# Norms and casts of three batches dealt anew between GpSimd and ScalarE, with a new written-out order

## The chip, the cores and the metric

The kernel runs on one core of one Trainium2 chip. The metric is device time in microseconds of one execution. The time of a kernel is the median of several runs; a profile is one further execution, taken by the hardware profiler.

The engines are named as the profile names them: PE is TensorE (matmuls; PEld is its loading of weights), DVE is VectorE, ACT is ScalarE, POOL is GpSimd, and SP is SyncE, which here only issues transfers. Each engine runs its instructions strictly in the order in which the program gives them, and waits at the head of its queue until what the next instruction needs is there.

## The reference, cut to what matters

```
# attention with forget gates: 8 batches, 8 heads, 576 positions, head size 64
scores = q @ k.T / 8
cum    = cumsum(log(clip(f, 1e-4, 1)))
scores = where(causal, -1e9, scores + cum[:, None] - cum[None, :])
attn   = exp(scores - max(scores))
attn   = attn / sum(attn)                  # the "norm" of this text
x      = attn @ v                          # -> 4608 tokens x 512
# bilinear feed-forward network
out    = ((x @ w_a) * (x @ w_b)) @ w_out   # 512 -> 1536 -> 512
```

All inputs and the output are fp32. The kernel works in fp16 with fp32 sums.

## The kernel before

**Work and tiles.** Heads are taken in pairs. A pair of heads of one batch is numbered `t` (0 to 31, four pairs to a batch), half a batch (two pairs) is `u` (0 to 15). The 576 rows of a pair fall into blocks of 128, `i` = 0 to 3, and a last block of 64 rows, `i` = 4. Scores are computed in groups: `groups = [(1, 0), (2,), (3,), (4,)]`, so that the operations `qk0` to `qk3` each make the scores of one group for one `u`.

**A pair's way.** The scores of a group are written by TensorE into PSUM (`sc`, L403). In batches 0 to 2 (`DIRECT = 3`) the decay is added by matmuls, VectorE takes the maximum of each row (`do_max`, L490) and ScalarE the exponential straight from PSUM (`do_exp`, L546 and L552), with its row sum; the next group reuses the banks of `sc`, so it waits for these exps. From batch 3 on VectorE adds the decay and takes the maximum in one instruction (`do_decay`, L514), reading a table that GpSimd masks (`mask_copy`, L464; `mask_tail`, L470; `mask_last`, L475). VectorE then takes the reciprocal of the sums (`do_recip`). The norm (`do_norm`, L569) multiplies the probabilities of one block and one head by it, in place, in the tile `PA` (blocks 0 to 2) or `PB` (3 and 4); `norm0` to `norm4` are its operations by block, two each, and one for block 4. Batch 0 isn't normed so: there the reciprocals are put across by small matmuls (`rhi` and `rlo` split them into two halves, `rmm` and `rev` spread them over rows) and multiplied in when the product with the values is read out. After its norms the tile is transposed by a transfer that SyncE issues (`do_tr`, L607, giving `PTA` and `PTB`), and TensorE multiplies it with the values (`pv`, `pv4`, `pve`; L635 to L660). In batch 0 TensorE does the transposes (`ptr`), and VectorE or ScalarE copy them out (`evp`).

**Inputs.** Queries, keys and values are loaded as fp32 by SyncE, cast to fp16 (`caqk`, `cav`), and queries and keys are transposed by VectorE (`tqk`, L304). In batch 0 the casts are shared out; from batch 1 on all are GpSimd's.

**Feed-forward.** Tokens are taken in blocks of 256 to 512. For each of 12 slices of the inner size TensorE makes `psa` and `psb` (L929), ScalarE or VectorE copies `psa` out (`aev`), and VectorE multiplies (`mul`, L945); `pso` (L954) is the second product, copied out by `ocopy` and stored by `sto` (L969). These matmuls are put between those of attention.

**What sets the order.** The program first lists all its work as 2307 operations, each with its function, the engines that it may run on (a string of letters: A for ScalarE, D for VectorE, P for GpSimd, S for SyncE) and what it depends on:

```
nm = op("P", f"norm{i}", lambda e, i=i, h=h: do_norm(e, t, i, h), [rc])
```

Then two texts decide: `ORDER` gives the sequence of the operations' numbers, and with it each engine's queue, and `CHOICE` gives one letter to each operation that has more than one engine to choose from. `laid_out` reads both. 40 matmuls without use (`fill`, L179) are part of the order; they keep TensorE at work.

Of the kernel before, what the change touches and what calls it, by code (L numbers as in the profile page):

```python
# [37 lines left out]
def kernel(  # L38
# [11 lines left out]
    nc = tc.nc  # L50
# [256 lines left out]
    def batch_inputs(b):  # L307
# [4 lines left out]
        for which, part, gm in items:  # L312
            gate = qk_ops[(2 * (b - 1) + gm // 4, gm % 4)][-1:] if b >= EARLY else []
            if which == "v":
                m, w = len(part), sbw[part[0]]
                ld = op("S", "ldv", lambda _, part=part: load_v(b, part), size=8 * m * w)
                ld.after.extend(gate)
                nu = take(ld, "n32")
                ca = op(("P" if 0 in part else "APD") if b == 0 else "P", "cav", lambda e, part=part: cast_v(e, b, part), [ld, o_p], 512 * m)
# [15 lines left out]
            for lo, hi in (((0, 5), (5, TW)) if b == 0 else ((0, TW),)):  # L335
                ca = op("APD" if b == 0 else "P", "caqk",
# [226 lines left out]
    def do_norm(e, t, i, h):  # L563
        st = T[("st", t)]
# [4 lines left out]
        ENG[e].tensor_scalar(out=p, in0=p, scalar1=st[:, c:c + 1], scalar2=1.0, op0=MUL, op1=MUL)  # L569
# [128 lines left out]
    def softmax(t, g, qk, sc, rows, st_users, pu, norms):  # L698
# [4 lines left out]
        for i in groups[g]:  # L703
# [67 lines left out]
            for h in range(1 if i == 4 else 2):  # L771
                nm = op("P", f"norm{i}", lambda e, i=i, h=h: do_norm(e, t, i, h), [rc])
# [261 lines left out]
    for t0, n in [(0, 256), (256, 256), (512, 256), (768, 384)] + [(1152 + 512 * n, 512 if n < 6 else 384) for n in range(7)]:  # L1034
# [3 lines left out]
        42-44 0 8 33 10 71 34 11 66 22 32 21 4 39 1 23 64 54 14 45-47 25 20 48 55-57 36 41 72-74 49 19 9 65  # L1038
        50 67-69 51 40 3 58 75-77 18 70 78 61 62 79-81 96 109 113 83 84 24 110 82 111 27 5 13 97 101 26 2 59
# [5 lines left out]
        198 199 173 178 150 180 179 174 176 175 286 230 185 287-289 299 214 305 87 88 200 177 300 306 207  # L1045
# [3 lines left out]
        369 233 238 229 195 1623 443 1624-1626 196 239 363 1627 1630 1632 279 370 1628 1629 236 371 1631 280  # L1049
        1634 1633 208 1636 364 365 258 284 275 259 281 285 244 245 237 388 393 209 372 389 290 292 394 291  # L1050
        282 283 445 1635 406 1638-1640 390 35 246 395 1637 1641 260 311 448 324 330 312 318 396 444 210 28
        201 202 247 366 261 325 326 211 1642 1643 314 264 266 267 327 320 319 265 1644 252 446 332 331 391
        333 313 321 322 373 315 203 204 349 356-358 392 329 253 350 352 351 367 250 449 1647 374 1648-1650
        347 251 303 1652 1654 375 382 353 1645 1653 1655 348 1656 1658 1657 1660 384 1662 328 1659 1661 1664
        1665 453 383 376 1663 1666-1668 1670 378 1669 1672 377 447 385 1674 1673 1671 1675 397 409 410 704
# [3 lines left out]
        476 478 495 477 386 504 454 455 506 505 1651 411 458 412 1700-1702 420 421 334 467 501 304 479 1703  # L1059
# [8 lines left out]
        615 552 607 547 1760 1763 1761 526 527 535 558-560 586 588 1764-1766 587 1768 1769 1772 1773 561 598  # L1068
        589 1774 1770 622 634 557 636 1771 1775 1776 1778 1777 1780 1781 667 674 642 546 675 708 604 1782
        1783 541 592 669 676 677 1784 1786 569 1779 581 641 580 594 1785 1787-1790 1792 563 643 562 593 635  # L1070
        591 585 590 605 606 608 678 644 595 645 646 637 668 609 638 640 639 1762 1793 1796 623 626 1794 602
        1795 627 1798 628 630 1791 647 670-672 631 648 650 681 683 1797 1799 1800 797 1801 1804 649 682 1802
        1803 651 652 684 620 632 655 1806 680 1805 679 1807 709 656 794 653 688 689 654 700 603 1808 1810
        1809 629 798 685 612 1812 1813 1816 1811 633 624 1817 657 658 1814 1815 1767 1818 1821 610 1822 690
        617 710 660 662 687 621 661 663 693-695 659 664 691 1819 673 696 697 686 702 712 724 732 731 757 765
        759 767 1823 1826 665 1827 726 764 1824 666 701 625 766 799 758 768 760 699 1828 698 692 703 795
# [12 lines left out]
        911 1906 966-968 925 926 915 927 914 918 931 933 916 917 935 904 959 961 1910 1010 919 969 970 936  # L1089
        1893 971 1014 972 1911 937 1912 1011 1915 973-975 1913 1914 938 920 1897 943 1003 939 960 1015 934  # L1090
        940 942 1012 928 976 977 1000 941 1916 1919 1921 944 905 1917 1920 1922 945 1016 912 913 909 1918
        921 946 1923 948 949 947 978-980 1898 990 1924 981 982 1927 1888 988 950 1100 951 952 1925 984 1929
# [97 lines left out]
```

## Time and profile before

| | |
|---|---|
| median of 3 runs | 403.02 us (402.19 to 403.34) |
| profiled execution | 401.62 us, of which the span from first to last instruction is 399.8 us |
| granted TensorE clock | 0.994 of full speed |
| busy PE, DVE, ACT, POOL | 385.3, 313.6, 252.1, 238.4 us |
| transfers | 78.21 MB, mean 196 GB/s |

A matmul's end is modelled in the profile, since matmuls overlap, so a busy TensorE need not be one at its peak. In the rows that name an instruction, `out<-in` are the tiles that it writes and reads, and the text in brackets or behind the last bar says for how long the engine had been idle before it and what ended that. A line such as L140 or L144 is that of the helper `cast` and stands for many uses.

### The profile page before, as it was taken

The numbers are of one execution on the slowest core, as the hardware profiler recorded it, in microseconds if no ns is written. First come the engines' busy times: TensorE is split into PE (matmuls) and PEld (weight loads), VectorE is DVE, ScalarE is ACT, GpSimd is POOL, SyncE is SP. The second block draws the span as 40 slices with busy tenths as digits, with TensorE's granted clock in tenths as the row PEclk, the third lists the DMA queues.
The fourth block names the chain that finished last, engine by engine and source line by source line (L and its number), as shares of the span: only waits on it lengthen the run. The fifth ranks groups of instructions, "written<-read, shape, count | busy, mean of one in ns | idle before, by whom it ended". The sixth has DMA issues, their size and how long they took to land.

```text
span 399.8 us, 10965 instructions
## 1 busy us (share of the span) xinstructions
PE 385.3 (96%) x4000; PEld 206.5 (52%) x4000; DVE 313.6 (78%) x915; ACT 252.1 (63%) x760; POOL 238.4 (60%) x401
## 2 busy tenths in 40 slices
PE   8888999999998999999999999999999999999996
PEld 2466876758655444444444454444444444444553
DVE  7999997978788979978988888899978891653361
ACT  6888986666565767767785677666868683201210
POOL 6461558896396877885886939768877563000000
PEclk9998999999999999999999999999999999999999
DMA  7999989999979999999999798999999827101102
GB/s 266 261 223 235 206 174 249 225 187 180 313 214 198 235 236 261 226 294 200 295 229 266 153 281 200 230 247 218 267 195 222 178 41 152 52 2 71 61 2 80
DMA packets 148310, 78.21 MB, mean 196 GB/s; under 512 B 130592, under 2 KB 133408, under 8 KB 148256
## 3 DMA queue, kind: packets, MB, share of 16 engines
q1 hardware_dynamic: 144560, 72.79, 78.9%
q0 software_dynamic: 3696, 4.72, 7.2%
q8 instruction: 31, 0.51, 0.5%
q14 instruction: 23, 0.19, 0.1%
HBM read 49.69 MB, written 9.58 MB: 148 GB/s over the span
## 4 chain that ended last, share of the span: by engine, by line
PE 62%; DMA 8%; DVE 8%; ACT 7%; POOL 7%; issue 5%; SPq 0%; POOLq 0%; DVEq 0%; ACTq 0%
PE pso L954 17%; PE psa L929 16%; PE psb L929 15%; PE sc L403 7%; DMA PTB<-PB 4%; DVE S L514 3%; POOL PB L569 3%; ACT PA L552 2%; DMA q<-in_q_dram 2%; POOL PA L569 2%; PE pv L635 1%; DMA spread<-cum_d 1%; DVE st L490 1%; PE pv L647 1%; ACT PB L552 1%
## 5 line engine op out<-in xcount | busy, mean ns | idle before, releaser
L929 PE MATMUL psa<-xT,wa 128*128 128x512 f16 (+2 forms) x528 | 115.6, 342 | 1.0 <-ACT a L140 0.5
L929 PE MATMUL psb<-xT,wb 128*128 128x512 f16 (+2 forms) x528 | 116.1, 343 | 0.0
L954 PE MATMUL pso<-wout,ht 128*128 128x512 f16 (+1 forms) x444 | 98.0, 374 | 0.0
L945 DVE TENSOR_TENSOR ht<-psb,a 128x512 f16<-128x512 f32 (+2 forms) x132 | 75.5, 588 | 22.6 <-PE psb L929 14.3
L569 POOL TENSOR_SCALAR PA<-PA,st 128x128 f16<-128x128 f16 (+2 forms) x150 | 70.1, 480 | 36.6 <-DVE st L561 27.4
L514 DVE CUSTOM_DVE_ANT_0 S<-sc,spread 128x128 f32<-128x128 f32 (+3 forms) x160 | 86.1, 569 | 4.3 <-PE sc L403 2.2
L552 ACT ACTIVATE PA<-S,st 128x256 f16<-128x256 f32 (+2 forms) x120 | 60.0, 502 | 21.8 <-DVE st L514 19.8
L929 PEld LDWEIGHTS <-wa 128*128 128x128 f16 x528 | 50.5, 98 | 44.8 <-issue 4.1
L140 ACT CAST a<-psa 128x512 f16<-128x512 f32 (+2 forms) x88 | 44.9, 517 | 44.9 <-PE psa L929 43.4
L929 PEld LDWEIGHTS <-wb 128*128 128x128 f16 x528 | 50.1, 98 | 42.0 <-issue 2.4
L954 PEld LDWEIGHTS <-ht 128*128 128x128 f16 x444 | 41.8, 98 | 47.4 <-issue 1.5
L569 POOL TENSOR_SCALAR PB<-PB,st 128x512 f16<-128x512 f16 (+1 forms) x78 | 54.5, 713 | 10.7 <-DVE st L561 6.6
L490 DVE TENSOR_REDUCE st<-sc 128x2 f32<-128x512 f32 (+8 forms) x68 | 46.6, 726 | 7.3 <-PE sc L403 7.2
L403 PE MATMUL sc<-kT,qT 32*128 32x128 f16 (+5 forms) x960 | 40.3, 268 | 4.0 <-ACT PA L552 2.1
L552 ACT ACTIVATE PB<-S,st 128x512 f16<-128x512 f32 x40 | 28.5, 714 | 6.0 <-DVE st L514 6.0
L403 PEld LDWEIGHTS <-qT 32*128 32x128 f16 (+1 forms) x960 | 18.7, 95 | 23.8 <-issue 13.5
L144 POOL CAST nv<-v 128x1024 f16<-128x1024 f32 (+1 forms) x24 | 21.3, 894 | 15.7 <-DMA v<-in_v_dram 15.7
L140 ACT COPY osb<-pso 128x512 f32<-128x512 f32 (+1 forms) x23 | 13.0, 571 | 25.1 <-PE pso L954 22.9
L144 DVE CAST a<-psa 128x256 f16<-128x256 f32 (+2 forms) x44 | 24.2, 551 | 5.7 <-PE psa L929 5.1
L561 DVE RECIPROCAL st<-st 128x2 f32<-128x2 f32 x128 | 18.1, 157 | 12.1 <-ACT PB L552 5.9
L142 POOL TENSOR_SCALAR q<-q 128x1152 f16<-128x1152 f32 (+1 forms) x15 | 20.9, 1395 | 8.8 <-DMA q<-in_q_dram 8.8
L552 ACT ACTIVATE PA<-sc,st 128x256 f16<-128x256 f32 (+2 forms) x42 | 19.6, 494 | 8.5 <-DVE st L490 3.6
(107 smaller groups left out, 485.3 us busy)
## 6 DMA issues: line engine op xcount, KB each, us to landing
spread<-cum_d SPq DMA_DIRECT2D x20, 576.0 KB, 6.0
out_dram<-osb SPq DMA_DIRECT2D x35, 256.0 KB, 3.6
q<-in_q_dram SPq DMA_DIRECT2D x15, 576.0 KB, 6.8
k<-in_k_dram SPq DMA_DIRECT2D x15, 576.0 KB, 7.5
v<-in_v_dram SPq DMA_DIRECT2D x32, 256.0 KB, 6.9
wout<-in_moe_w_out_dram POOLq DMA_DIRECT2D x3, 512.0 KB, 8.9
wa<-in_moe_w_a_dram POOLq DMA_DIRECT2D x1, 1024.0 KB, 11.7
v<-in_v_dram SPq DMA_DIRECT2D x8, 128.0 KB, 5.3
```

What stands on the lines that cost most here:

```text
L140: nc.scalar.copy(out=out_, in_=in_)
L142: ENG[e].tensor_scalar(out=out_, in0=in_, scalar1=0.125, scalar2=1.0, op0=MUL, op1=MUL)
L144: ENG[e].tensor_copy(out=out_, in_=in_)
L403: nc.tensor.matmul(out=dst, lhsT=lhsT, rhs=rhs, start=start, stop=stop, skip_group_check=True)
L490: nc.vector.tensor_reduce(out=m if i == 4 else st[:, 2 * i:2 * i + 2][:, h:h + 1] if isinstance(x, list) else m, in_=y, axis=AXX, op=MAX, ...
L514: nc.vector.tensor_tensor_reduce(out=o, in0=x, in1=y, scale=-1.0, scalar=3e38, op0=ADD, op1=MIN, accum_out=m)
L552: nc.scalar.activation(out=p_blocks(t, i)[:, :, h, :], in_=x.rearrange("p (j k) -> p j k", k=128), func=EXP, scale=sign, bias=st[:, c:c + ...
L561: nc.vector.reciprocal(out=st[:, 20 + 2 * i:22 + 2 * i], in_=st[:, 10 + 2 * i:12 + 2 * i])
L569: ENG[e].tensor_scalar(out=p, in0=p, scalar1=st[:, c:c + 1], scalar2=1.0, op0=MUL, op1=MUL)
L929: nc.tensor.matmul(out=o, lhsT=w16[:, db, 128 * fb:128 * fb + 128], rhs=tokens(db, t0, n), start=(db == 0), stop=(db == 3))
L945: nc.vector.tensor_tensor(out=ht[:, 0:n], in0=T.pop(("psb", t0, fb))[:, 0:n], in1=T.pop(("a16", t0, fb))[:, 0:n], op=MUL)
L954: nc.tensor.matmul(out=o, lhsT=T[("ht", t0, fb)][:, 128 * tb:128 * tb + 128], rhs=wout16[:, fb, c], start=(fb == 0), stop=(fb == 11))
```

## The change

The norms of batches 1 and 2 may now run on ScalarE or GpSimd, and so may the casts of batches 1 to 3. `do_norm` gets a branch for ScalarE: a copy with the reciprocal as its scale. `ORDER` and `CHOICE` are new texts; the orders agree from a point in batch 5 on. By the letters of `CHOICE`:

- 16 of the norms are given to ScalarE: for `t` = 4, 5, 6, 7 one, two, three and three; for `t` = 8, 10 and 11 two, two and three. By block they are two `norm0`, five `norm1`, four `norm2`, four `norm3` and one `norm4`.
- Of the casts, one goes to ScalarE: the last 64 rows of the values of batch 3.
- 15 copies of `psa` go from ScalarE to VectorE and 6 from VectorE to ScalarE. Of the read-outs of products with the values (`ev`, `ev4`, `eve`) five go from ScalarE to VectorE and eight the other way. Two `ocopy` change places in each direction, two `rev` go to ScalarE and one to VectorE, one `evp` goes to VectorE. Of the halves of reciprocals of batch 0, three `rlo` and two `rhi` go from GpSimd to VectorE, two `rhi` from VectorE to ScalarE, one from VectorE and one from ScalarE to GpSimd.
- In the order of the transfers one store comes ahead of the first query load of batch 3, and the two decay loads of batch 3 (`ldb`) change places.

```
-                ca = op(("P" if 0 in part else "APD") if b == 0 else "P", "cav", ...
+                ca = op(("P" if 0 in part else "APD") if b == 0 else "PA" if b < 4 else "P", "cav", ...
...
-                ca = op("APD" if b == 0 else "P", "caqk",
+                ca = op("APD" if b == 0 else "PA" if b < 4 else "P", "caqk",
...
-        ENG[e].tensor_scalar(out=p, in0=p, scalar1=st[:, c:c + 1], scalar2=1.0, op0=MUL, op1=MUL)
+        if e == "A":
+            nc.scalar.activation(out=p, in_=p, func=COPY, scale=st[:, c:c + 1])
+        else:
+            ENG[e].tensor_scalar(out=p, in0=p, scalar1=st[:, c:c + 1], scalar2=1.0, op0=MUL, op1=MUL)
...
-                nm = op("P", f"norm{i}", lambda e, i=i, h=h: do_norm(e, t, i, h), [rc])
+                nm = op("PA" if b < 3 else "P", f"norm{i}", lambda e, i=i, h=h: do_norm(e, t, i, h), [rc])
...
     ORDER = """   (new text; the first 1418 of 2307 places differ)
...
     CHOICE = """   (new text)
```

More of the change, by code (lines that the diff above doesn't have):

```diff
@@ L318, in batch_inputs @@
                 nu = take(ld, "n32")
-                ca = op(("P" if 0 in part else "APD") if b == 0 else "P", "cav", lambda e, part=part: cast_v(e, b, part), [ld, o_p], 512 * m)
+                ca = op(("P" if 0 in part else "APD") if b == 0 else "PA" if b < 4 else "P", "cav", lambda e, part=part: cast_v(e, b, part), [ld, o_p], 512 * m)
                 nu.append(ca)
@@ L1051 @@
[L1051 to L1055, printed above, removed]
[3 rows of a table removed]
@@ L1072 @@
[L1072 to L1076, printed above, removed]
@@ new lines @@
+        115 101 114 98 103 99 11 102 33 10 20 6 121 122 66 83 84 126 128 268 146 124 104 127 16 123 24 90
+        134 138-140 147 135 269 226 136 151 152 227 153 149 89 116 100 14 31 155 105 137 112 148 117 129 156
+        157 141 142 164 158 160 162 125 161 143 91 169 212 213 254 255 240 170 171 118-120 271 165 272 144
+        145 241 234 235 166 167 52 53 262 263 130-133 92 273 63 248 249 276 220 106-108 221 93 182-184 18
+        1594 190 191 1596 1595 1597 1598 1600 270 1599 168 1602 1604 150 1601 216 217 159 197 205 206 7 198
@@ new lines @@
+        199 173 178 180 179 286 1603 1606 174-176 287 293 1607 185 186 299 305 214 187 95 288 289 294 300 85
[4 rows of a table added]
+        371 236 364 365 237 366 285 258 259 282 244 245 368 292 388 346 348 1633 393 394 389 1634-1636
+        1638-1640 1637 1641 390 391 210 211 202 260 261 311 324 330 312 332 326 325 372 246 331 318 283 445
[3 rows of a table added]
+        384 1655 1659-1661 1664 1665 376 1666 1662 1663 1668 1670 341 456 383 1667 1669 385 387 1672 1674
+        1673 378 377 379 1671 1675 321 397 402 406 403 398 399 1676 1678 342 1677 1680-1682 316 1684 303
@@ new lines @@
+        1679 1683 404 417 422 460 423 1685 1688 492 498 1686 1687 1689 1690 493 494 499 500 705 464 470 465
+        471 472 1692 1693 1691 1694 1695 38 409 410 466 405 310 1696-1698 408 28 501 467 469 381 416 413 414
+        495 618 400 1651 461 476 478 477 1699 504 505 450 506 420 507 380 457 458 1700 1701 479 407 1702 411
+        412 473 462 1703 454 474 482 483 510 455 434 317 1705-1707 386 511 329 335 1708 421 323 322 424 427
+        428 463 433 436 437 435 415 418 419 502 438-440 401 441 512 451 452 17 484 486 488 514 1710-1712
@@ new lines @@
+        646 700 611 661 663 659 691 692 1822 694 696 664-666 1767 799 695 697 712 757 724 732 725-727 734
+        701 699 698 703 1819 795 796 1823 1826-1828 625 759 765 767 1831 1824 764 766 1833 728 730 729 758
+        731 733 768 769 1832 1835 1836 1834 713 716 1837 717 720 714 715 721 1838-1840 735 737 736 738 739
+        760 761 740 771 772 805 806 741 1841 1842 718 719 802 803 816 773 742-744 722 762 810 745 746 707
+        774-776 1843 778 779 711 763 777 1844 1847 1845 1846 1848 770 747 748 1849 749 1850 812 723 750 1820
@@ new lines @@
+        1080-1083 1052 1053 1013 1084 1085 1102 1017 1054 1952 1005 1086 1087 1953 1954 1957 1076 1029 1025
[5 rows of a table added]
+        1136-1138 1115 1140 1141 1133 1164 1166 1169 1989 1201 1212 1213 1142 1196 1170 1171 1210 1991 1993
+        1992 1174 1165 1173 1143 1198 1175 1172 1103 1995 1996 1990 1107 1126 1119 1997 1999 2000 1998 1144
+        1176 1177 1146 1148 2001 1139 1994 1147 1178 1966 1179 1180 1214 1145 1149-1152 2002 2003 2005 2004
+        1188 1182 2007 1181 1183 2009 1185 1956 1216 1261 1228 1269 1184 1229 1262 2006 2008 2011 2013 2010
@@ new lines @@
+        2012 2014 1197 1230-1232 1235 2015 2016 1233 1199 1186 1268 1237 1187 1263 1270 1264 2017 2018 1236
+        2020-2022 1189 1238 1200 1271 1272 1202 1203 1221 1217 1239 1240 1224 2023 1220 1265 1266 1222 1267
+        1225 1223 1275 2025 1242 1243 1274 1298 1299 1244 1245 1276 1278 1206 1207 2026 1241 1300 1273 1218
+        2019 1226 1246 1247 1388 1219 1249 1248 1250 1277 1279 1281 1211 1204 2027 1282-1284 2028 2030 2031
+        2024 1234 1215 2032 1302 2033 1304 1280 1285 1286 1251 1227 1287 1303 1288 1391 1289 1254 1255 1290
@@ new lines @@
+        1291 1293 1292 2035 2036 1294 2039 2040 1306 1256 1257 2037 2038 1252 1253 1258 1260 2041 2042 1318
+        1259 1326 1320 1328 1351-1353 2043 2044 1358 2047 2049 1325 2045 1319 2046 2048 2051 2053 2052 1392
+        2055 1359 2050 1393 2054 1361 2056 2059 1360 1296 1297 1389 1390 1205 1321 1362-1364 2057 2058 1354
+        1311 1327 1329 1314 1322 1324 1295 1307 1330 1310 1308 1309 1410 1315 1332 2060 2063 1396 2061 1333
+        1335 1312 1334 1365-1367 1355 1356 2062 1316 1336 1323 2064 1372 2067 2065 1357 1338 1399 2034 1373
[3 rows of a table added]
@@ new lines @@
+        1407 1386 1401 1426 1434 1433 1397 1398 2083-2085 2088 2089 2086 1385 2090 2093 2094 1462-1464 1427
+        1415 1418 1387 1419 1428 1435 1420 1496 2091 2092 1422 1468 1470 1471 1436 1437 1439 1438 1402 1429
+        1430 1432 1421 1431 1423 1497 1440 1442 1473-1475 1500 1441 1443 1444 2095 2098 1416 1465 1412 1472
+        1424 1480 1408 1476 1477 1479 1478 1447 2099 2100 1448 1481 1409 2096 1417 2103 2105 1501 2087
+        1449-1451 1482 2104 2106 1413 2101 1394 1425 1452 1454 1453 1485 1486 1445 1446 2107 2108 1455-1458
[4 rows of a table added]
@@ new lines @@
+        2132 2135 2137 1522 1506 1507 2134 1566 1529 1514 2136 2139 2141 1498 1537-1539 1534 2140 2143
+        1570-1572 1515 2142 1567 1536 1554 2138 1540 2144 2147 2148 1499 2145 1542 1544 1535 1582 1569 1543
+        2151 2152 1503 1575 1576 1545 1546 2146 2149 1578 2150 1562 2153 2156 2157 1577 2154 1568 2158 2161
+        2159 1555 2162 2163 1541 2166 2167 1588 1579 1548 1547 1583 1585 1586 1580 1573 1581 1574 1589 1591
+        2160 2168 1592 2169 2171 2173 2170 2172 2174 2175 2177 2176 2178-2180 2164 2165 2181-2183 2185 2184
@@ new lines @@
+        2186-2188 2191 2189 2190 2193 1584 1590 1593 2192 2195 2197 1587 2196 2198 2199 2194 2201 2200 2202
+        2203 2205 2204 2207 2208 2206 2211 2213 2209 2210 2212 2215-2220 2214 2221-2223 2155 2224-2227 2229
+        2230 2228 2231 2234 2232 2233 2235-2239 2241 2240 2242 2243 2245 2244 2246-2249 2251 2250 2253 2252
+        2254-2256 2259 2261 2257 2260 2263 2262 2258 2264-2273 2275 2277 2276 2279 2274 2280 2283 2281 2282
+        2284-2287 2278 2288-2290 2292-2294 2297 2298 2291 2295 2296 2299 2302-2306 2300 2301
@@ L1145 @@
+        ADDDAADAAADADAADAADDADDDAADAADDDDDADDADADADAAADDDDADADADAAAAAADAAADDDADAAAAAADADDAAAADAADAAADADADADD
+        AAADDAAAAAAAADADADAADADAAAAAAAAAADAAADADAAAAAAADAADDADADDDAAADDAAAADADAADDADDDAASDS
     """
```

66 lines of the change are left out of this document (14 added, 52 removed), and 82 rows, old and new, of the table ORDER.

## The prediction

> **What bounds the kernel now.** I read the page's first part, then its slices, then busy time by stretch, then what TensorE waited for, then the chain around the largest wait.
>
> ```profile
> PE 385.3 (96%) x4000; PEld 206.5 (52%) x4000; DVE 313.6 (78%) x915; ACT 252.1 (63%) x760; POOL 238.4 (60%) x401
> PE   8888999999998999999999999999999999999996
> ...
> 0.00:41.80 41.80, 34.79 (x509) 21.08 (x509) 37.99 (x96) 34.67 (x112) 18.97 (x37) 0.96 1.04 244
> ...
> 45.20:78.70 33.50, 33.44 (x565) 24.61 (x563) 29.02 (x76) 25.48 (x77) 25.82 (x41) 1.00 1.06 206
> 78.70:115.00 36.30, 35.77 (x567) 23.77 (x566) 28.73 (x70) 23.44 (x82) 25.19 (x43) 1.00 1.06 238
> 115.00:139.90 24.90, 23.40 (x225) 12.99 (x223) 22.27 (x72) 17.31 (x54) 19.49 (x33) 1.00 0.98 203
> 139.90:240.00 100.10, 98.89 (x915) 46.27 (x914) 85.54 (x287) 71.66 (x216) 76.13 (x127) 1.00 1.06 244
> ```
>
> TensorE is busy 385.3 of 399.8 us. No matmul is added, dropped or made shorter, so the change can win only from the other 14.5 us, or lose by adding to them. The stretches (from, to, length, then busy time of PE, PEld, DVE, ACT, POOL, then clock and DMA) place them: 7.0 idle us before 41.8, almost none to 78.7, 0.5 to 115, 1.5 to 139.9, 1.2 to 240, and the rest behind, mostly at the tail. The two orders are the same from a score group of batch 5 on (215 us here), so only what lies before can move, and a shift made there is carried to the end by a TensorE without slack.
>
> ```profile
> PE sc L660 <- DMA PTB<-PB: 2.5, 4, 1.0
> PE sc L403 <- ACT PA L552: 2.1, 3, 1.3
> ...
> PE psa L929 <- ACT a L140: 0.5, 2, 0.3
> ```
>
> Of TensorE's own waits (total us, times, longest), the 2.1 us for ScalarE's exps all lie in the first 41.8 us. The 2.5 us for PTB are transposes by DMA of normalised probabilities, the product of the norms that the change moves. So the gain to look for is there.
>
> **The moved work.** Reading the letters against the operations: 16 norms go from GpSimd to ScalarE (9 of batch 1, 7 of batch 2; two norm0, five norm1, four norm2, four norm3, one norm4) and one 64x512 value cast of batch 3. No row shows a norm on ScalarE; the nearest are its exps of the same tiles, which also take a scale and a bias per row.
>
> ```profile
> L569 POOL TENSOR_SCALAR PA<-PA,st 128x128 f16<-128x128 f16 x50 | 18.5, 373 | 18.4 <-DVE st L561 11.2 <-issue 6.4 <-POOL nv L144 0.7
> L569 POOL TENSOR_SCALAR PA<-PA,st 128x256 f16<-128x256 f16 x50 | 23.7, 482 | 8.3 <-DVE st L561 6.8 <-issue 1.5
> L569 POOL TENSOR_SCALAR PA<-PA,st 128x384 f16<-128x384 f16 x50 | 29.0, 587 | 9.9 <-DVE st L561 9.4 <-ACT PB L546 0.4
> L569 POOL TENSOR_SCALAR PB<-PB,st 128x512 f16<-128x512 f16 x52 | 35.5, 695 | 9.3 <-DVE st L561 6.6 <-DVE st L559 2.5
> L569 POOL TENSOR_SCALAR PB<-PB,st 128x576 f16<-128x576 f16 x26 | 19.4, 748 | 1.4 <-DVE st L559 1.3
> ...
> L552 ACT ACTIVATE PA<-S,st 128x128 f16<-128x128 f32 x40 | 15.7, 393 | 1.7 <-DVE st L514 1.7
> L552 ACT ACTIVATE PA<-S,st 128x256 f16<-128x256 f32 x40 | 20.1, 504 | 10.8 <-DVE st L514 9.1 <-POOL PB L569 1.5
> L552 ACT ACTIVATE PA<-S,st 128x384 f16<-128x384 f32 x40 | 24.3, 609 | 9.3 <-DVE st L514 9.0
> L552 ACT ACTIVATE PB<-S,st 128x512 f16<-128x512 f32 x40 | 28.5, 714 | 6.0 <-DVE st L514 6.0
> L546 ACT ACTIVATE PB<-S,st 128x576 f16<-128x576 f32 x20 | 15.5, 775 | 9.8 <-POOL PA L569 6.8 <-DMA v<-in_v_dram 1.1 <-DVE st L514 0.9
> ```
>
> GpSimd loses 2x0.373 + 5x0.482 + 4x0.587 + 4x0.695 + 0.748 = 9.0 us, ScalarE gains 2x0.393 + 5x0.504 + 4x0.609 + 4x0.714 + 0.775 = 9.4 us. The engines are equally fast; what is bought is balance. In 45.2 to 115 ScalarE is idle 8.0 + 12.9 = 20.9 us, so I put the 9.4 us at nothing on the path. If that cover is gone at one place, one norm that stands ahead of an exp in ScalarE's queue costs 0.39 to 0.78 us, because the next score group needs the banks that those exps read. A norm there also waits for its reciprocal from VectorE with the exps queued behind it. Bounds: 0 to nine norms of batch 1 at about 0.55, 5 us; I take 0, since the idle time is twice the moved work.
>
> **The wait for PTB, where the gain should be.**
>
> ```profile
> 101.60 0.47 SPq L969 DMA_DIRECT2D out_dram<-osb  x1
> ...
> 105.35 1.40 POOL L142 TENSOR_SCALAR q<-q 128x1152 f16<-128x1152 f32 x1 [5.32 <-DMA q<-in_q_dram]
> ...
> 110.44 1.40 POOL L144 CAST k<-k 128x1152 f16<-128x1152 f32 x1 [1.61 <-DMA k<-in_k_dram]
> ...
> 115.94 0.69 ACT L552 ACTIVATE PB<-sc,st 128x512 f16<-128x512 f32 x1
> ...
> 117.33 2.75 POOL PB L569 x4
> ...
> 120.58 5.97 DMA PTB<-PB
> ...
> 125.30 0.35 PE L660 MATMUL sc<-PTB,nv 128*64 128x64 f16 x10 [0.55 <-DMA PTB<-PB]
> 126.60 0.35 PE L660 MATMUL sc<-PTB,nv 128*64 128x64 f16 x10 [0.95 <-DMA PTB<-PB]
> ...
> L464 POOL TENSOR_SCALAR_AFFINE_SELECT spread<-spread 128x768 f32<-128x768 f32 x20 | 17.4, 868 | 6.9 <-DMA spread<-cum_d 6.9
> ```
>
> This is the largest steady wait: TensorE stands 0.55 + 0.95 us until the transposes of pairs 10 and 11 have landed. GpSimd had stood 5.32 us behind the query cast of batch 3, then worked without a break from 111.80, when its next instruction after the key cast began, to 120.08. In the new order GpSimd's queue after that key cast holds three norm0, one norm1, one norm2, three norm3, two norm4 and two mask copies: 3x0.373 + 0.482 + 0.587 + 3x0.695 + 2x0.748 + 2x0.868 = 7.5 us against the 8.3 us now. The last norm3 goes to ScalarE. So the second transpose can start 0.8 us sooner. It can't gain more: the last exp of the group starts at 115.94, and that hangs on the score group, not on GpSimd. In SyncE's queue the order of those four transposes stays. The store that took 0.47 us to issue at 101.60 is now ahead of the query load of batch 3, so that load and its cast can come 0.47 us later; the key load, which GpSimd waits for next (1.61 us), has two small issues ahead of it beside the query load in both orders, so the key cast keeps its time and nothing of the 0.8 goes to the store. Bounds: 0 (mask copies or the query load late) and -1.5, both waits gone; I take -0.8, what the queue gives. The waits for PTB behind 139.9 belong to pairs whose norms don't move: 0.
>
> **VectorE, where a loss can come from.** Evictions are dealt anew: 15 copies of the first product go from ScalarE to VectorE and 6 back. Between the last maximum of the second score group of batch 1 and that of the first group of batch 2 (45.2 to 78.7) VectorE's queue gains five such copies, three reciprocals, two low parts from GpSimd, one copy of transposed blocks and one value eviction, and loses two row copies.
>
> ```profile
> L144 DVE CAST a<-psa 128x256 f16<-128x256 f32 x18 | 7.5, 416 | 1.4 <-PE psa L929 1.3
> L561 DVE RECIPROCAL st<-st 128x2 f32<-128x2 f32 x128 | 18.1, 157 | 12.1 <-ACT PB L552 5.9 <-ACT PA L552 5.5
> L144 DVE COPY PTB<-psP 128x640 f16<-128x640 f16 x1 | 0.5, 492 | 0.0
> L144 DVE COPY rb<-psr 128x320 f32<-128x320 f32 x2 | 1.0, 488 | 0.2 <-PE psr L586 0.2
> L577 POOL TENSOR_TENSOR r<-st,r 128x5 f16<-128x5 f32 x4 | 0.8, 195 | 0.3
> ...
> DVE st L490 <- PE sc L403: 2.5, 5, 0.8
> ...
> 47.91 1.22 DVE L490 TENSOR_REDUCE st<-sc 128x2 f32<-128x1024 f32 x1 [0.35 <-PE sc L403]
> ```
>
> That is 5x0.416 + 3x0.157 + 2x0.195 (GpSimd's row; VectorE has none) + 0.492 + 0.416 - 2x0.488 = 2.9 us, against 4.5 us in which VectorE is idle there, 2.5 of them waiting for scores. In this phase scores go TensorE to VectorE (maximum) to ScalarE (exp) and back, and the next group waits for that. The first step is the tight one: two of the five copies (0.83 us) now stand before the maximum that starts at 47.91, where VectorE has 0.35 us to spare. So +0.45 us; the other three fall where the waits for scores are. Bounds 0 and +2.9.
>
> **The rest.** Up to 34 us ScalarE's queue to the exps of batch 0's last groups is the same work in another order, and three more idle matmuls stand there, in time that TensorE waits anyway: 0 (-0.5, the earlier maxima, to +0.6, the idle matmuls uncovered). Of the 0.5 us of waits for copies, 0.2 lie behind 41.8; moved copies can remove them: -0.2 (0 to -0.2). VectorE's further five copies at 139.9 to 206 lie in a stretch with 14.6 idle us: 0.
>
> Sum: -0.8 + 0.45 - 0.2 = -0.55 us. The profiled execution took 401.62 us (span 399.8 and 1.8 around it), so 401.1. It was faster than any of the three runs shown (402.19 to 403.34); against their median of 403.02 the same sum gives **402.5 us**. That is no change within the 0.3% (1.2 us) below which this kernel's runs tell nothing.
>
> [...]
>
> ```profile
> 33.33:36.74 3.41, 1.94 (x56) 1.50 (x53) 3.41 (x8) 3.11 (x9) 0.35 (x1) 1.00 1.14 211
> 36.74:40.16 3.42, 3.42 (x22) 2.52 (x21) 3.05 (x12) 3.42 (x15) 1.33 (x4) 0.50 1.14 282
> ```
>
> After 3.41 us in which TensorE was busy 1.94, its clock was granted at 0.50 for the next 3.42 us. It cost little, as ScalarE was busy for all of those 3.42 us and the next score group waited for it. The same 3.4 us at half clock among dense matmuls would cost 1.7 us. [...]
>
> **The rivals.**
> - Faster, 0.34. All four waits for PTB go (2.5 instead of 0.8): 402.5 - 1.7 = 400.8 us. For: GpSimd's queue is some 9 us shorter by 115 us. Against: only two of the four belong to pairs whose norms move.
> - Slower, 0.24. VectorE becomes the bound from 45 to 79 us: its 2.9 us find no cover in the loop of scores. Then +2.9 instead of +0.45, 404.9 us; it decides from 2.1 us uncovered. For: VectorE is busy 87% there. Against: half of its idle time is waiting for TensorE.
> - A half-clock window falls on dense matmuls, 0.05: 402.5 + 1.7 = 404.2 us, at the edge of no change.
> - No change by the sum, 0.37.
>
> The two last hold the 0.42 of no change. The range goes from 400.0 (400.8, less the 0.5 and 0.2 that the start and the copies may give) to 405.0 (VectorE's 2.9 uncovered).
>
> **What would show it.** Right: the norms on ScalarE within 5% of 0.39 to 0.78 us; the wait of the matmuls for PTB near 125 us down by 0.8 us, the others kept; VectorE busier by about 2.5 us between 45 and 79 us; TensorE busy the same. Wrong: TensorE waiting for ScalarE's exps after 42 us (a norm ahead of an exp), a second stretch of clock 0.50, or GpSimd still standing long at the mask copies of batch 3.

## The result, and the profile after

The changed kernel took 405.84 us (median of 20 executions, 403.31 to 411.11), the kernel before 403.54 us beside it on the same chip (20 executions, 401.12 to 405.54). The ratio is 1.0058, with a 95% interval of 1.0036 to 1.0080: 2.3 us slower, where 402.5 us and no change had been predicted. Executions of one kernel lie up to 8 us apart, so single times say little here; the ratios say how much, and the profile of one execution shows where. A ratio leaves out disturbed executions, so it can differ a little from that of the medians.

The profiled execution took 405.2 us. Its busy times, and the stretches that answer to those shown of before:

```profile
PE 386.7 (96%) x4000; PEld 206.2 (51%) x4000; DVE 316.0 (78%) x923; ACT 258.0 (64%) x772; POOL 227.8 (56%) x381
...
45.20:78.70 33.50, 33.40 (x559) 24.45 (x557) 30.08 (x85) 27.65 (x82) 21.81 (x35) 1.00 1.05 218
78.70:115.00 36.30, 35.37 (x569) 23.68 (x569) 28.14 (x65) 27.32 (x91) 20.34 (x33) 1.00 1.02 224
115.00:139.90 24.90, 24.33 (x250) 13.38 (x248) 22.83 (x73) 18.79 (x57) 19.44 (x31) 1.00 1.08 209
```

Work did move: GpSimd is 10.6 us less busy in all (238.4 to 227.8), ScalarE 5.9 us more. TensorE's idle time in 115 to 139.9 fell from 1.5 to 0.57 us. So far the change did what it was meant to. To find where the time went I took the start of the same score group in both traces and subtracted; the shift is negative where the changed kernel is earlier. A shift also moves when the new order puts other matmuls between two groups, so the last row gives TensorE's idle time as well, summed from the two traces.

| score group, its start before | 95.6 | 117.0 | 127.4 | 171.0 | 219.5 | 225.3 | 256.4 | 277.6 | 325.9 |
|---|---|---|---|---|---|---|---|---|---|
| shift in the changed kernel, us | -1.06 | +0.87 | -0.69 | +0.39 | +0.31 | +1.33 | +2.44 | +3.43 | +3.63 |
| TensorE idle since the group to the left, before / changed, us | 6.00 / 5.46 | 0.24 / 0.72 | 1.50 / 0.57 | 0.52 / 1.73 | 0.69 / 0.21 | 0.00 / 0.63 | 0.15 / 1.29 | 0.29 / 0.98 | 0.07 / 0.08 |

Up to 140 us the kernel is 0.7 us ahead. The 1.9 us between 95.6 and 117 are mostly order and no loss: in the changed kernel eight more `psa` matmuls (48 against 40) and one `fill` stand between these two groups, and four fewer from there to 127.4 (20 against 24). What is lost up to 117 is idle time, 0.72 us against 0.24. Up to 127.4 the 1.50 us of waits for PTB are gone, and a new wait of 0.57 us stands in their place. TensorE's waits from 100 to 125 us in the changed kernel (total us, times, longest):

```profile
PE pso L957 <- DVE ht L948: 0.6, 1, 0.6
PE psb L932 <- ACT a L140: 0.6, 1, 0.6
```

Between 127.4 and 171 us TensorE gets 1.2 us more idle time, which comes up again with theory B below. And 3.3 us are lost behind 219.5 us, 2.5 of them idle time, although from 220 us on every engine's queue holds the same work in the same order as before. TensorE's waits there in the changed kernel (208 to 275 us):

```profile
PE sc L403 <- DVE st L514: 0.9, 2, 0.6
PE psb L932 <- DVE ht L948: 0.7, 1, 0.7
PE sc L403 <- DVE xT L144: 0.6, 1, 0.6
PE psa L932 <- DVE a L144: 0.3, 1, 0.3
```

L514 adds the decay biases to a score; TensorE waits for it to give the score's banks back. Why it is late stands in GpSimd's timeline of the changed kernel (start, length, instruction, idle time before it and its releaser), with VectorE's and TensorE's rows behind it:

```profile
214.09 1.04 POOL L144 CAST nv<-v 128x1024 f16<-128x1024 f32 x1 [1.74 <-DMA v<-in_v_dram]
215.08 0.29 POOL L470 TENSOR_SCALAR_AFFINE_SELECT spread<-spread 128x128 f32<-128x128 f32 x1
...
217.86 0.60 POOL L144 CAST nv<-v 64x512 f16<-64x512 f32 x1 [2.02 <-DMA v<-in_v_dram]
...
218.88 0.29 POOL L470 TENSOR_SCALAR_AFFINE_SELECT spread<-spread 128x128 f32<-128x128 f32 x1
...
221.62 0.40 POOL L475 TENSOR_SCALAR_AFFINE_SELECT spread<-spread 128x256 f32<-128x256 f32 x1
...
219.20 0.75 DVE L514 CUSTOM_DVE_ANT_0 S<-sc,spread 64x576 f32<-64x576 f32 x1 [1.04 <-POOL spread L470]
...
220.79 0.60 PE L403 MATMUL sc<-kT,qT 32*128 32x512 f16 x6 [0.63 <-DVE st L514]
```

The L470 instructions cut the causal mask into the last 128 columns of the biases of tiles 20 and 21 (`mt`, operations 1012 and 1016). In the kernel before they ran at 197 and 199 us, ahead of both value casts:

```profile
197.09 0.29 POOL L470 TENSOR_SCALAR_AFFINE_SELECT spread<-spread 128x128 f32<-128x128 f32 x1
...
198.73 0.29 POOL L470 TENSOR_SCALAR_AFFINE_SELECT spread<-spread 128x128 f32<-128x128 f32 x1
...
214.34 1.04 POOL L144 CAST nv<-v 128x1024 f16<-128x1024 f32 x1 [3.27 <-DMA v<-in_v_dram]
...
216.24 0.60 POOL L144 CAST nv<-v 64x512 f16<-64x512 f32 x1
...
219.29 0.40 POOL L475 TENSOR_SCALAR_AFFINE_SELECT spread<-spread 128x256 f32<-128x256 f32 x1
```

They moved 18 and 20 us later, behind two casts of batch 5's values that wait for their loads. The second load is late as well: SyncE now issues batch 6's first query load (operation 1193) ahead of it. None of this is long in itself: a tail takes 0.3 us. It changed its place in a queue. The L475 row shows the effect: GpSimd reaches it 2.3 us later than before.

TensorE's new wait for `ht`, at 109 us, has the same form on VectorE. Changed kernel:

```profile
106.06 1.40 POOL L142 TENSOR_SCALAR q<-q 128x1152 f16<-128x1152 f32 x1 [4.51 <-DMA q<-in_q_dram]
...
107.50 1.22 DVE L304 STREAM_TRANSPOSE qT<-q 128x576 f32<-128x576 f32 x1 [1.54 <-POOL q L142]
108.57 0.40 DVE L144 CAST a<-psa 128x256 f16<-128x256 f32 x1
...
109.08 0.42 DVE L948 TENSOR_TENSOR ht<-psb,a 128x256 f16<-128x256 f32 x1
```

VectorE stands 1.54 us before the transposes of batch 3's query, which wait for its cast and so for its load, with the copy and the multiply of slice 11 behind them (operations 1756 and 1757); TensorE's second product needs that `ht` and waits 0.6 us for it. Before, the copy stood ahead of the transposes, and VectorE reached them at 106.83, when the cast of 105.35 had just ended, without a wait.

### The profile page after: what moved, and what is told of

It reads as the page before. It is cut to its first block, busy times and chain, and to the rows that moved or that the text cites. A ratio compares the mean times of both kernels' runs of the same rounds, so it can differ in the third digit from the quotient of the medians.

```text
span 403.4 us, 10962 instructions
## 1 busy us (share of the span) xinstructions
PE 386.7 (96%) x4000; PEld 206.2 (51%) x4000; DVE 316.0 (78%) x923; ACT 258.0 (64%) x772; POOL 227.8 (56%) x381
## 5 line engine op out<-in xcount | busy, mean ns | idle before, releaser
L514 DVE CUSTOM_DVE_ANT_0 S<-sc,spread 128x128 f32<-128x128 f32 (+3 forms) x160 | 86.3, 568 | 8.5 <-PE sc L403 3.9
L572 POOL TENSOR_SCALAR PA<-PA,st 128x256 f16<-128x256 f16 (+2 forms) x143 | 66.3, 475 | 42.3 <-DVE st L561 24.8
L140 ACT CAST a<-psa 128x512 f16<-128x512 f32 (+2 forms) x79 | 40.5, 518 | 41.7 <-PE psa L932 41.0
L572 POOL TENSOR_SCALAR PB<-PB,st 128x512 f16<-128x512 f16 (+1 forms) x76 | 53.0, 710 | 9.5 <-DVE st L561 5.0
L490 DVE TENSOR_REDUCE st<-sc 128x2 f32<-128x512 f32 (+7 forms) x68 | 46.5, 724 | 8.4 <-PE sc L403 8.1
L403 PE MATMUL sc<-kT,qT 32*128 32x128 f16 (+5 forms) x960 | 41.2, 270 | 4.1 <-ACT PA L552 1.5
L144 DVE CAST a<-psa 128x512 f16<-128x512 f32 (+2 forms) x53 | 29.2, 554 | 4.7 <-PE psa L932 3.8
L552 ACT ACTIVATION_READ_ACCUMULATOR PA<-S,st 128x1 f32 x120 | 22.6, 188 | 0.0
```

The costliest lines, as they stand in the source:

```text
L140: nc.scalar.copy(out=out_, in_=in_)
L144: ENG[e].tensor_copy(out=out_, in_=in_)
L403: nc.tensor.matmul(out=dst, lhsT=lhsT, rhs=rhs, start=start, stop=stop, skip_group_check=True)
L490: nc.vector.tensor_reduce(out=m if i == 4 else st[:, 2 * i:2 * i + 2][:, h:h + 1] if isinstance(x, list) else m, in_=y, axis=AXX, op=MAX, ...
L514: nc.vector.tensor_tensor_reduce(out=o, in0=x, in1=y, scale=-1.0, scalar=3e38, op0=ADD, op1=MIN, accum_out=m)
L552: nc.scalar.activation(out=p_blocks(t, i)[:, :, h, :], in_=x.rearrange("p (j k) -> p j k", k=128), func=EXP, scale=sign, bias=st[:, c:c + ...
```

## The experiments

Each is the changed kernel, or the one before, with a few operations at another place or on another engine. Theory A: the loss is made by the queues of GpSimd and SyncE at 205 to 222 us. Theory B: by the evictions that went to VectorE at 155 to 215 us. Theory C: by the norms in ScalarE's queue. Theory F came later: by VectorE's place for the query transposes at 107 us. Ratios are to the kernel before, run beside it on the same chip. The experiments ran on three chips, so medians from different ones are best compared by their ratios.

| kernel | median, us | ratio (95% interval) |
|---|---|---|
| changed | 405.84 | 1.0058 (1.0036 to 1.0080) |
| + mask tails put back | 404.32 | 1.0026 (0.9997 to 1.0056) |
| + SyncE's load put back | 404.71 | 1.0026 (0.9993 to 1.0058) |
| + both | 402.71, again 404.76 | 0.9985 (0.9964 to 1.0006), 1.0022 (0.9990 to 1.0053) |
| + VectorE's edit alone | 404.37 | 1.0027 (0.9996 to 1.0058) |
| + all three | 401.96, again 401.94 | 0.9958 (0.9931 to 0.9984), 0.9969 (0.9938 to 1.0000) |
| + all three, query load first | 402.50 | 0.9996 (0.9961 to 1.0032) |
| + six evictions put back | 405.74 | 1.0071 (1.0041 to 1.0101) |
| + norms (and the value cast) put back | 420.45 | 1.0444 (1.0397 to 1.0492) |
| new first part, old rest | 405.15 | 1.0036 (1.0001 to 1.0072) |
| the same + VectorE's edit | 402.25 | 0.9988 (0.9955 to 1.0021) |
| old first part, new rest | 403.97 | 1.0012 (0.9984 to 1.0040) |
| before + norms (and the value cast) on ScalarE | 443.44 | 1.0993 (1.0950 to 1.1037) |
| before + VectorE's edit | 403.00 | 1.0005 (0.9975 to 1.0036) |

**The mask tails alone.** In `ORDER` of the changed kernel:

```
- 1945 1946 999 989 ... 1036 1067 1007 1012 1069 1078 1008 1009 1035 1016 1947
+ 1945 1946 1012 1016 999 989 ... 1036 1067 1007 1069 1078 1008 1009 1035 1947
```

> The changed kernel with one edit: GpSimd's two tail copies of the masks of tiles 20 and 21 (mt of t=20 and 21) stand ahead of batch 5's value casts in GpSimd's queue again, as before; engines and all other orders are the changed kernel's. Theory A (the loss behind 215 us comes from GpSimd's queue, where these tails, run at 197.1 and 198.7 us before, now wait behind two value casts and run at 215.1 and 218.9): the stall of 1.02 us at 221 goes, and most of the 3.3 us lost between 215 and 280 with it: 1.0 to 3.0 us faster than the changed kernel's 405.8, so 402.8 to 404.8. Theory B (the loss is made at 157 to 168 us, where VectorE has no idle time and took over output evictions): the shift of TensorE at 171 stays near +0.4 and the time at 405.5 or above. Theory C (ScalarE's norms hold up its exps): 405.8, no change.

1.5 us less at the median, though the intervals of the two ratios overlap. The shift is -0.75 us at both 219.5 and 225.3: the stall at 221 is gone, as theory A had it. But 1.05 us are still lost between 225.3 and 256.4. GpSimd still stands 2.2 us before the late value load there, but that this is the cause isn't shown: the first profile with all three edits (below), in which GpSimd has no such wait before its second value cast, loses 0.74 us over the same stretch.

**Tails and load.** In addition:

```
- 1006 1004 1193 1077 ... 1104 1888
+ 1006 1004 1077 ... 1104 1193 1888
```

> As the experiment on the two mask tails, and one more edit: in SyncE's queue the load of batch 6's q (first half) stands behind batch 5's last value load and the bias load of tile 23 again, as before. Theory A with the transfers as the second half of the cause (the value casts wait 1.74 and 2.02 us for their loads): GpSimd no longer stands before the value casts at 214 and 218 us, and the time falls by a further 0.3 to 1.0 us below the kernel with the tails alone. If only the order on GpSimd counts: the same time as that kernel. Theories B and C: 405.8, no change.

In its profile nearly the whole loss behind 219.5 us is gone, 0.5 us instead of 3.3: shift -0.34 at 219.5, -0.53 at 256.4, +0.20 at 325.9. GpSimd's second value cast no longer waits, and the line that ended in 2.02 us of waiting reads

```profile
215.52 0.60 POOL L144 CAST nv<-v 64x512 f16<-64x512 f32 x1
```

The first median, 402.71, agreed with the profile; the second, from a later experiment, did not:

> The kernel with the two mask tails and SyncE's load put back, again, unchanged. If its 402.7 was no accident: a median of 402.2 to 403.2, at or under the kernel before in the same call. If it was: 403.5 to 405, beside the two kernels with one edit each (404.3, 404.7).

404.76: the first was probably luck in part, though it also ran on another chip. The profile of the second loses 2.5 us between the score groups of 95.6 and 117 (shift +0.24 to +2.75), with 1.1 us of TensorE idle, where the first lost 1.6 (-0.80 to +0.81), with 0.4 us idle. So something besides theory A costs time, in some executions more than in others, and at a place that I had read as a detail.

**SyncE's load alone**, the tails left behind the casts:

> The changed kernel with only SyncE's edit: the load of batch 6's q (first half) stands behind batch 5's last value load and tile 23's bias load again; the two mask tails stay behind the value casts on GpSimd. If the late value load is what makes the tails late (GpSimd waits 2.02 us for it at 217.9 us): most of the stall at 221 us goes and the time is 402.7 to 404. If the order on GpSimd alone counts: 405 to 406, no change.

404.71. The stall at 221 us is gone in its profile too (-0.18 at 219.5, -0.17 at 225.3), with the tails still late, at 215.23 and 216.95. Either edit removes that stall: it needs both, the tails behind the casts and the late load. The median lies between the two forecasts, so this run alone would not have decided.

**Six evictions back** (operations 1829, 1873, 1877, 1892, 1901, 1937 with the letters of before):

> The changed kernel with the six output evictions and copies of 155 to 215 us that changed engine (fb 10 and 11 and the copy of block 2 of t0=1152, the copy of block 2 of t0=768, fb 0 and 9 of t0=1664) back on the engine that had them before; the order stays. Theory B: TensorE's shift from 160 to 171 us (+2.1 us of step, from -1.75 to +0.39) does not happen, 1.0 to 2.0 us faster than the changed kernel; the stalls at 221, 247, 259 and 271 us stay. Theory A: the first step shrinks by at most 0.5 us and the time by no more. Theory C: no change.

405.74, and the step from 161 to 171 us stays (-2.06 to -0.24). Theory B falls. A part of that step is order: four `psa` matmuls (0.9 us) that stood ahead of the group of 156.9 before now stand between 161 and 171, which is also why the shift falls by 1.0 us on the way to 156.9. The rest is idle time of TensorE, 1.73 us against 0.48 between these two groups, with two waits that the kernel before does not have (changed kernel):

```profile
163.71 1.02 PE L932 MATMUL psa<-xT,wa 128*128 128x512 f16 x4 [0.37 <-DVE ht L948]
165.46 1.02 PE L932 MATMUL psb<-xT,wb 128*128 128x512 f16 x4 [0.73 <-ACT a L140]
```

Both are in the profile of every kernel that has the new order of this part, 0.4 and 0.7 us, also of the ones that came out fastest, and with the six letters put back they are 0.51 and 0.73 us. The two kernels with the new first part and the old rest don't have the second and only 0.2 us of the first. So the order makes them; which operations do isn't settled, and no run tried to take them away.

**The norms back on GpSimd**, and the reverse, **the norms alone on ScalarE** in the order of before:

> The changed kernel with its 16 norms and the one value cast of batch 3 back on GpSimd, each at its place in the order. Theory C (ScalarE's norms delay what it does for TensorE): 1 to 3 us faster than the changed kernel. Theories A and B: no gain from it; GpSimd gets 9.4 us of work back before 160 us, the waits of TensorE for transposed scores near 125 us (0.55 and 0.95 before, gone after) may return: 0 to 1.5 us slower.

> The kernel before with one edit: the 16 norms and the value cast that the change gave to ScalarE run on ScalarE, each at its place in the order of before; all else is of the kernel before. If the moved work costs and wins nothing by itself (as the prediction had it): 402.5 to 403.5. If GpSimd's relief is what made the waits for the transposed scores near 125 us go: the two of them (0.71 and 1.14 us) shrink and the time is 0.5 to 1.5 us below before. If norms in ScalarE's queue hold up its exps at places that no one chose for them: 404 to 406.

420.45 and 443.44 us: both far outside of every expectation. The moved work is 9.4 us. In the first, SyncE's queue waits for the late norms with the other transposes behind them (70 to 135 us; its waits for norms come to 27.1 us there, the longest 13.2, and to 17.6 us in the kernel before, the longest 7.2):

```profile
SPq L610 <- POOL PB L572: 20.9, 5, 13.2
SPq L274 <- POOL nv L144: 8.8, 1, 8.8
```

and in the second for the norms on ScalarE (whole span):

```profile
SPq L610 <- ACT PA L570: 32.5, 4, 14.7
...
SPq L610 <- ACT spread L570: 18.4, 4, 6.1
```

A place in `ORDER` isn't a time. A norm (operation 334) that GpSimd ran at 74.5 us, as it was ahead of the order there, ran on ScalarE at 87.8 us, because ScalarE's queue reached that place only then. Its transpose came late, then TensorE, then the read-outs that ScalarE makes ahead of its next norm: a loop through the queues of ScalarE, SyncE and TensorE, in which TensorE stands 3 to 6 us a turn. The loop is read from who waited for whom; no run cut it. These two runs can't decide theory C, as they make a worse loop than the one that they were to remove. What speaks against it is the runs above and below, in which the loss goes while all norms stay on ScalarE. The order and the engines can only be judged together.

**New first part with the old rest, and the reverse.** The text is cut behind 963 operations (about 142 us):

> Engines and order of the changed kernel for its first 963 steps (to about 142 us, with all 16 norms and the value cast on ScalarE), the engines and order of the kernel before for the rest. Theory A (the change wins 0.7 us up to 140 us and loses 3 us or more by queue orders behind 215 us): no stall at 221 us, no loss behind 171 us beyond that of the kernel before, and time 0.0 to 0.7 us below the kernel before (402.3 to 403.0 beside 403.0). Rival D (VectorE, without idle time at 157 to 168 us, gives back whatever was won before it): the shift of -0.7 us at 140 us is near 0 at 171 us, and the time is that of the kernel before within 0.3 us. Rival E (the norms on ScalarE cost something later on): 1 us or more slower than before.

> The reverse: engines and order of the kernel before for its first 963 steps (to about 143 us, all norms on GpSimd), those of the changed kernel for the rest. Theory A: the loss needs none of ScalarE's norms: the stall near 221 us and those at 247, 259 and 271 us are there, and the time is 3.0 to 4.5 us above the kernel before (406 to 407.5). Rival E: within 1 us of the kernel before.

405.15 and 403.97: theory A's numbers (402.3 to 403.0, and 406 to 407.5) fail both ways. The reverse does show the stalls behind 215 us without a norm on ScalarE: shift +0.08 at 219.5, +1.43 at 225.3, +2.21 at 277.6. But more of the loss seems to come with the new first part, 0.36% against 0.12% (the intervals overlap), which the changed kernel's own profile had shown as a gain. The first hybrid's profile tells why (VectorE, TensorE and GpSimd at 105 to 111 us):

```profile
106.83 1.40 POOL L142 TENSOR_SCALAR q<-q 128x1152 f16<-128x1152 f32 x1 [5.72 <-DMA q<-in_q_dram]
...
108.26 1.21 DVE L304 STREAM_TRANSPOSE qT<-q 128x576 f32<-128x576 f32 x1 [2.75 <-POOL q L142]
109.32 0.41 DVE L144 CAST a<-psa 128x256 f16<-128x256 f32 x1
...
109.83 0.42 DVE L948 TENSOR_TENSOR ht<-psb,a 128x256 f16<-128x256 f32 x1
...
110.31 1.25 PE L957 MATMUL pso<-wout,ht 128*128 128x512 f16 x5 [1.82 <-DVE ht L948]
```

The same steps as in the changed kernel, with the load 0.8 us later; VectorE waits 2.75 us and TensorE 1.82 us. That became theory F.

**VectorE's edit in the hybrid.**

```
- 1755 1758 569 1753 600 1759 576 550 549 551 601 547 1756 577 573 1757 530
+ 1755 1758 569 1753 600 1759 576 550 549 551 1756 1757 601 547 577 573 530
```

> The kernel with the changed first part and the old rest, with one edit on VectorE: the eviction of output-gate block 11 of t0=512 and its multiply stand ahead of the transposes of batch 3's first q half, which wait for its cast and so for its load. Theory F (that hybrid is 405.2 because VectorE waits for q with TensorE's next eviction queued behind it: 2.00 us lost at 110.5 in its profile, 0.49 to 0.80 in other executions of the same steps, after a load that takes longer in some executions): the stall at 110 us is under 0.4 us and the median falls by 1 to 3 us to 402.2 to 404.0. If the loss is somewhere else (behind the cut, or by ScalarE's norms): the stall shrinks in the profile and the median stays within 0.7 us of 405.2.

402.25: a ratio of 0.9988, where the hybrid had 1.0036 on another chip. Its profile caught the cast that waits for the load later still, and that costs TensorE nothing:

```profile
107.06 1.40 POOL L142 TENSOR_SCALAR q<-q 128x1152 f16<-128x1152 f32 x1 [4.95 <-DMA q<-in_q_dram]
...
107.34 0.42 DVE L948 TENSOR_TENSOR ht<-psb,a 128x256 f16<-128x256 f32 x1
108.50 1.22 DVE L304 STREAM_TRANSPOSE qT<-q 128x576 f32<-128x576 f32 x1 [0.73 <-POOL q L142]
...
109.06 1.90 PE L957 MATMUL pso<-wout,ht 128*128 128x512 f16 x8
```

The multiply is done at 107.76, before the transposes, and the second product at 109.06 starts without a wait. With the multiply behind VectorE's wait of 2.75 us, 1.82 us were passed on to TensorE; with the multiply ahead of it, none. The multiply did not pass the transposes that waited, in the changed kernel either: there TensorE had ended its last `psb` at 104.88, VectorE stood idle for 1.54 us up to 107.50, and the copy and the multiply still ran behind the transposes, at 108.57 and 109.08.

**All three edits in the changed kernel**, twice, and with the query load of batch 3 ahead of an output store on SyncE (`599 1709` for `1709 ... 599`):

> The changed kernel with the two mask tails and SyncE's load put back (402.7 in its first run) and VectorE's edit of the last experiment. Theory F: the stall of 0.49 us at 109.7 goes, 0.0 to 0.6 us faster than that kernel: 402.1 to 402.7, and faster than the kernel before. Otherwise the same as that kernel.

> The changed kernel with the mask tails and SyncE's load put back and VectorE's edit, again, unchanged. If it is faster than the kernel before: a median of 401.3 to 402.5 and a ratio of 0.994 to 0.998 to it. If its first run was luck, as was the 402.7 of the kernel without VectorE's edit: 402.5 to 404.

> As the last one, and on SyncE batch 3's q load ahead of the output store that the changed order put in front of it. If the store ahead delays the load: q's cast on GpSimd starts 0.5 to 1 us earlier (106.0 before the edit) and the time falls by up to 0.3 us more. If the transfer's own length sets it: no difference.

401.96 and 401.94: ratios 0.9958 and 0.9969, so 1.7 and 1.2 us faster than before, the second interval just reaching 1. The profiles do not show where this gain is made: TensorE is idle about as long as before, and the first of the two still loses 1.7 us behind 219.5 us (shift -0.58 to +1.15; the second 0.6), though the stall at 221 us is gone in both. This is the version to keep: the change as made, with five operations (1012, 1016, 1193, 1756, 1757) at another place. Moving the query load as well did start its cast earlier (105.56 instead of 106.47 and 105.96), but the time was 402.50, not better; TensorE has no wait near 109 us either way, so the load is hidden.

**VectorE's edit alone**, in the changed kernel and in the one before (there the multiplies 1753 and 1757 go ahead of 601):

> The changed kernel with VectorE's edit alone (eviction and multiply of block 11 of t0=512 ahead of the transposes of batch 3's first q half); the queues behind 200 us stay as changed. If the orders on SyncE and GpSimd at 205 to 222 us (theory A) and VectorE's wait for q (theory F) each cost their part: 403.5 to 405, between the changed kernel (405.8) and the kernel with both mended (402.0), with the stall near 221 us still in the profile. If theory F is nearly all of it: 402 to 403. If theory A is nearly all: 405 to 406.

> The kernel before with VectorE's edit alone: the multiplies of blocks 10 and 11 of t0=512 stand ahead of the transposes of batch 3's first q half (the eviction of block 11 does so already). Theory F says the kernel before loses there in executions in which the load is late (0.42 us at 109.2 in its profile): 0 to 1 us faster, 402 to 403. If VectorE's order there matters only in the changed kernel: no difference from before.

404.37 in the changed kernel, with the stall at 221 us still there (shift -0.35 at 219.5, +0.42 at 225.3): as forecast, between the changed kernel and the one with all three. In the kernel before it does nothing (1.0005). Single intervals reach 0.2 to 0.4% to either side, so most single steps are not clear of noise; taken together they are. Four pairs of runs differ in VectorE's edit alone (the changed kernel, the kernel with tails and load put back twice, the first hybrid): their mean ratio is 1.0025 without it and 0.9986 with it, a difference of 0.4% with about 0.2 to either side. The kernels with tails and load both put back have 0.9984 in the mean, with and without VectorE's edit, and the same without these two edits 1.0043: 0.6%, again with about 0.2. So that the loss has these two causes, at 107 and at 205 to 222 us, is shown, and removing them leaves a gain; how the second is split between the tails and the load isn't. The profiles agree on the first, weakly: from the score group of 95.6 to that of 127.4 the seven executions of the new first part as made, without VectorE's edit, lost 0.07 to 1.58 us on the kernel before, the five with the edit at most 0.07.

## Why the prediction was wrong, point by point

- **The norms on ScalarE cost what the exps' rows said.** 0.39 to 0.78 us was predicted by size, within 5%. The changed kernel's rows:

```profile
L570 ACT ACTIVATE PA<-PA,st 128x384 f16<-128x384 f16 x3 | 1.7, 608 | 0.0
L570 ACT ACTIVATE PA<-PA,st 128x256 f16<-128x256 f16 x3 | 1.6, 525 | 0.0
L570 ACT ACTIVATE PB<-PB,st 128x512 f16<-128x512 f16 x2 | 1.5, 753 | 0.2 <-DVE st L561 0.2
```

  That is 0.608 against 0.609, 0.525 against 0.504, 0.753 against 0.714 us (5.5% over). They cost nothing on the path that the trace shows: ScalarE hardly waits before them, and TensorE has no new wait for exps behind 42 us. "I put the 9.4 us at nothing" held at the places chosen. The bound of 5 us for a misplaced set was far too low: 17 and 40 us.
- **The wait for PTB near 125 us** went wholly (0.55 + 0.95 us to none), where -0.8 was taken. But TensorE's idle time in that stretch fell by only 0.93 us, since 0.57 us of a new wait for a copy of `psa` came in at 120 us. So the net came out near -0.8, though not by the prediction's sum.
- **The waits for copies** were taken at -0.2. They grew instead: behind 41.8 us TensorE waited 0.5 us for ScalarE's copies of `psa` before and 1.6 us in the changed kernel (0.57 at 120 us, 0.73 at 165 us). It isn't the norms that hold up these two: ScalarE had been idle 1.11 and 1.48 us ahead of them, waiting for TensorE's `psa`. (Only one of the two waits of before, 0.2 us, lies between 41.8 and 240 us; the other is behind 240, not ahead of 41.8.) This term had the wrong sign. It stays in the kernel that came out faster, so it isn't what the three edits mended.
- **VectorE at 45.2 to 78.7** got 1.06 us busier, not 2.9, and TensorE lost nothing there (idle 0.10 us, 0.06 before). The term of +0.45 was about 0.
- **Failed step 1: the query load of batch 3.** The prediction saw the store ahead of it and said "so that load and its cast can come 0.47 us later", and went on to weigh that against GpSimd's 0.8 us alone. It did not ask who waits for the cast. VectorE does, and the new order had put a copy and a multiply that TensorE needs behind that wait. The cast came 0.71 us later (105.35 to 106.06), and TensorE waited 0.6 us for the multiply in the changed kernel's profile, 1.8 in the hybrid's. By the ratios this place costs about 0.4%. The queue order on VectorE from 104 to 110 us was not compared.
- **Failed step 2: "only what lies before can move, and a shift made there is carried to the end".** TensorE's order is the same from 200 us on, but GpSimd's is only from 220 us, and the engines enter the common part in another state. GpSimd entered it 2.3 us late (its L475 instruction of tile 20 ran at 221.62 instead of 219.29), and behind 219.5 us TensorE lost 3.3 us in that profile. With the tails and the load back in place about 0.6% of the time returns. The prediction had no term for GpSimd's or SyncE's queue at 205 to 222 us; the tails had gone past 18 us of other work and were not seen.
- **VectorE's five copies behind 139.9 at 0** held only as far as the letters go: putting six evictions back gained nothing. The new order of that stretch did cost: 1.2 us more of TensorE's idle time between 127.4 and 171 us, for which the prediction had no term.
- **The rivals.** "All four waits for PTB go" came nearest in mechanism: 2.5 us of them became 0.8. "VectorE becomes the bound" gave a time (404.9) nearer to what was measured, by a mechanism that did not happen: VectorE was not too busy, it stood in the wrong place of its queue. Neither named a wait of one queue on a load. (The lower end of the range is 0.1 off: 400.8 less 0.7 is 400.1, not 400.0.)
- **The clock**: 1.00 in each of the stretches behind 41.8 us, so no second stretch at half speed shows.

## What to carry to other kernels

Where engines take their work in order, as in these traces, compare each queue of the two versions operation by operation, and ask of every operation that waits for a load what has been put behind it; the busy time moved says little. A part of the program whose text is unchanged isn't unchanged if an engine enters it late, so look for operations that went far in their queue, however short. When a new order is a little slower, look for the few operations behind a load before giving it up: here five moved places turned a loss of 0.6% into a gain of 0.3 to 0.4%.

## What the runs showed of the hardware

The queues were worked in the order of the program. In the profiles of the kernel before and of the changed one the source lines of VectorE's 915 and 923 instructions, of ScalarE's 760 and 772 and of SyncE's 191 transfers come in the sequence that `ORDER` gives, and so do those of GpSimd's 388 and 368 beside the 13 that set up constants and load weights. TensorE's 4000 matmuls do so operation by operation in the changed kernel; within a `pv` they come in other pairs than the source has them, and in the kernel before one matmul of a `pv4` starts 0.03 us ahead of the last one of the `pv` in front of it (169.40 and 169.43 us), so its order is not strict to the single matmul.

One load took a different time in two executions of the same program, 5.9 and 7.2 us. In the two profiled executions of the kernel with all three edits SyncE issued batch 3's query load at

```profile
100.60 0.43 SPq L290 DMA_DIRECT2D q<-in_q_dram  x1
```

and

```profile
98.80 0.43 SPq L290 DMA_DIRECT2D q<-in_q_dram  x1
```

The casts that waited for it began at 106.47 and 105.96, that long after the issue. Over all kernels with the new first part it was 5.6 to 7.5 us. An order in which such a load has no slack can get a slower median with little sign of it in the profile of one execution: the changed kernel's own profile showed the first part as a gain.

In one run a low clock came with the long stalls. With the norms alone on ScalarE (from, to, length, busy time of PE, PEld, DVE, ACT, POOL, then clock):

```profile
100.00:105.00 5.00, 0.00 (x0) 0.00 (x0) 1.23 (x2) 0.17 (x1) 0.04 (x1) 0.84 0.65 125
105.00:110.00 5.00, 4.92 (x47) 3.75 (x47) 0.93 (x3) 3.82 (x11) 0.71 (x2) 0.50 0.00 0
```

From 100 to 105 us no matmul ran; in the next 5 us TensorE was busy for 4.92 at a granted clock of 0.50. The mean clock of that execution was 0.95, against 0.996 in the changed kernel. Its span is 44.0 us longer than that of the kernel before: TensorE's busy time rose by 14.3 us (385.3 to 399.6) for the same 4000 matmuls, and its idle time by 29.7. So the stalls themselves are two thirds; the low clock can account for the other third (an estimate: 0.05 of 443.8 us is 22 us, a part of it idle time), which no run separated from the modelled ends of the matmuls.
